# A block of constant products in front of the second head pair's cluster assignment, in place of 16 filling products

## Chip, cores and metric

The kernel runs on one core of a Trainium2 chip. The metric is the device time of one execution in microseconds (us). The kernel before takes 649.86 us (median of 3 executions, 649.46 to 650.00).

## What is computed

Two attentions, one after the other. The first has 4 batches of 8 heads, 768 tokens, head size 64; tokens are assigned to one of 16 clusters by their largest product with normalised centroids, and a query sees only the keys of its own cluster. The second is a causal attention with four experts on the result, of which two are weighted into each token. Cut to what matters here:

```
q_assign = argmax(einsum('bhsd,hcd->bhsc', q_n, c_n), -1)   # k_assign likewise
mask   = q_assign[:, :, :, None] == k_assign[:, :, None, :]
scores = where(mask, scale * q @ k.T, -1e9)
attn   = exp(scores - max(scores)); attn /= sum(attn) + 1e-9
x      = attn @ v                                            # then the four experts on x
```

## The kernel before, in words

The work goes by pairs of heads: 16 pairs of the clustered attention (n = 0 to 15), then 8 of the expert attention. For one pair:

- q and k (tiles `acc`, `xh`, `xl`, `kt`, `qt`, by pair) are loaded and turned so that the head size lies on partitions: by TensorE transposes (L476) for the first pairs, by VectorE transposes (L468) later; ScalarE copies them out (L320) into `xk`, `xq` or, for the second pair, `xh2`, `xh3`.
- **Assignment** (L507): four products of 128 rows and 32 columns of the array write the cluster scores of q and k into one tile of `pp`. VectorE then turns them (L511), takes the maximum, compares and ranks (L518 to L526) and turns back (L514); ScalarE makes rows of it (L531), which go by DMA into `tk`. All of this happens in place in the `pp` tile, so that tile is held until L526 has read it.
- **Row maxima** (L848 products in 64 and 48 rows of the array, two of them side by side; VectorE reduces them at L862): 12 groups of four products for a pair, in two halves of six; each half ends in a small reduce (L868), a turn (L878) and a DMA into `tk`.
- **Scores** (L915), exponentials on ScalarE (L921), sums on GpSimd and VectorE (L325, L326), products with v (L959).

`pp` is PSUM: four slots of two banks each, and every tile of PSUM takes one. `tk0` to `tk2` and `tq0` to `tq2` hold the operands of three pairs in turn.

The order is written out by hand. Work is recorded as numbered operations; the table `ORDER` lists them in the order in which they are issued, each engine runs its own in that order, and `~32` stands for 32 filling products (`spin`, L1103: 128 columns on a tile of ones, result unused). `SLOTS` gives each buffer its slot. In the table before, the filling products stand in rows of 34, 12, 17, 32 and 38 in the first 17 us. The first pair's row maxima begin behind the last of them.

Of the kernel before, what the change touches and what calls it, by code (L numbers as in the profile page):

```python
# [18 lines left out]
FT = mybir.dt.float32  # L19
# [13 lines left out]
          m_add=4, m_moe=0, m_xt=1, enter=4.0)  # L33

ORDER = """
0 4 32 31 33 ~34 1 3 2 56 ~12 8 145 5 10* 9* 13* 6 7 17* 14 ~17 20 18* 34 21 22 37 38 239 36 39 23 35 41 24 147 25 ~32
45 40 28 60 46 11 47 29 15* 27 30 12* 55 48 16* 61 62 42* 44 49 ~38 78 68 79 50 70 76 54 51 71 74 238 69 72 75 57 77
58 89 59 73 52 93 63 91 80 87 81 65* 90 82 88 85 53 43* 94 83 19 86 144 109 84 112 110 92 100 64 159 113 103 333 160
101 98 95 104 163 106 99 164 155 102 107 161 157 146 115 96 158 105 97 240 426 162 108 119 116* 156 111 153 120 332
125 154 117 126 172 118 170 173 122 121 165 131 171 123 128 241 132 124 129 134 166 167 135 136 127 557 137 114 138  # L40
# [99 lines left out]
1220330320332010021313200331111210221220313301322023330012131022133320011001230111020032320323021032032101201203233112  # L140
2210310302011200213321330111301332210023011310023202233323203011102012012133123312010220220122310300323312201003031201
1333331320211101231200030221122002033211201031001230030103301120312022231322011232132200222311300203221210013320231010
3112033030330002212233111133012113001120330010300000000000000000000000010110010101001001010100110010100000000000000000
0000000000000000101010101010101000000000000000000000000000000000000000000000000000000000000000000000000000000000010101
0101010101101010101010101010101010010101010101010101010101010101010101101010101010010101010101010101010100000000000000
0000000000000000000000000000000000000000000000000000000000000000000000000000000000000000000000000000000000000000000000
0000000000000000000000000000000000000000000000000000000000000001201201201201201201201200000000000000000000000000000000
0000000000000000000000000000000000000000000000000000000000000000000000000000000000000000000000000000000000000010101010
1010101010101010000000000000000000000000011000101101011010101010100101110000110100000101000101000000000000000001230123
"""  # L150


# [30 lines left out]
class Plan:  # L183
# [11 lines left out]
    def op(self, eng, dur, fn, due, after=(), use=(), lat=0.0, mode=128, alt=None, at=0.0, port=False):  # L195
        o = Op(eng, dur, fn, due, after, use, lat, mode, alt, at, port)
        self.needs(o, after, use)
        self.ops.append(o)
        return o
# [51 lines left out]
def t_mm(n):  # L251

    return n / 2400 + 0.016
# [13 lines left out]
def kernel(  # L267
# [14 lines left out]
    PE, ACT, DVE, POOL, SP = nc.tensor, nc.scalar, nc.vector, nc.gpsimd, nc.sync  # L282
    B, H, S, D = q.shape
# [4 lines left out]
    HW = S // 2  # L288
# [18 lines left out]
    op = plan.op  # L307

    def dma(dst, src, e=SP):
        e.dma_start(*[x.bitcast(FT) if x.dtype == FR else x for x in (dst, src)])  # L310

    def issues(moves):
        return [(x[0] + 0.045 + 0.05 * (i == 0),) + x[1:] for i, x in enumerate(moves)]

    def banks():
        return plan.buf(psum, "pp", (128, 2, 512), FT, 4)

    def copy_op(dst, src, n, due, after, use, sbuf=False):

        return op("act", t_act(n, sbuf), lambda: ACT.activation(dst(), src(), AF.Copy), due, after, use,  # L320
                  alt=(MO["m_copy"], "dve", t_dve(n), lambda: DVE.tensor_copy(dst(), src())), port=sbuf)  # L321
# [12 lines left out]
    def tmp(tag, shape, dt=FT, bufs=1):  # L334
        return plan.buf(sb, tag, shape, dt, bufs)
# [58 lines left out]
    TK, TQ = [], []  # L394
# [14 lines left out]
    def base(n):  # L409
        return AT["pair"] * min(n, NA) + MO["pair"] * max(n - NA, 0) + \  # L410
            (AT["first"] if n == 0 else AT["second"] if n == 1 else 0.0)
# [654 lines left out]
    def moe_out(b):  # L1066

        n = NA + b * EP + EP - 1
        t1 = base(n) + MO["pair"] + MO["out"]
        wh, wl = W["wo"]  # L1070
        for c in range(NC):
            final = n == NS - 1
            late = final and c >= HC
            m = banks() if c % 2 == 0 else m
            ot = tmp("rb", (128, DM)) if final and c == NC - 1 else tmp("vt" if late else "xt", (128, DM), bufs=2)
            due = base(n) + 40 + c if final else t1 + MO["out_step"] * c
            o = None
            for ep in range(EP):
                d = P[n - EP + 1 + ep]
                if "hl" in d:  # L1080
                    (ah, al_), ready = d["hl"], d["a"][c // HC]
                else:
                    ah, al_, ready = d["a"]

                def go(m=m, c=c, ep=ep, ah=ah, al_=al_):
                    ts = slice(c * 128, (c + 1) * 128)
                    for i, (a_, w_) in enumerate(((ah, wh), (ah, wl), (al_, wh))):
                        PE.matmul(m()[:, c % 2], a_()[:, ts], w_()[:, ep, :], start=(ep == 0 and i == 0),  # L1088
                                  stop=(ep == EP - 1 and i == 2))
                o = op("pe", 3 * t_mm(DM), go, due + 4 * (late and ep == EP - 1), [ready, o] + W["wo_ready"],  # L1090
                       [m, wh, wl, ah, al_, ot])

            o = copy_op(ot, lambda m=m, c=c: m()[:, c % 2], DM, due + 2, [o], [m, ot])

            def go(ot=ot, c=c):
                dma(out[b, c * 128:(c + 1) * 128, :], ot())
            op("sp", issues([(0.36, 0.65, 1.4)]), go, due + 3, [o], [ot])
# [24 lines left out]
    for n in range(NA, NS):  # L1122
# [8 lines left out]
        if ep == 0 and b:  # L1131
            moe_out(b - 1)
    moe_out(B - 1)
    plan.run()


# [26 lines left out]
```

## Time and profile before

| | before |
|---|---|
| median of 3 executions | 649.86 us |
| the profiled execution | 649.03 us |
| its span, first to last instruction | 647.0 us |
| TensorE busy, mean granted clock | 635.7 us, 0.994 |
| VectorE, ScalarE, GpSimd busy | 479.6, 301.1, 457.7 us |

Busy time is what the records cover; idle time of an engine that is not the bound costs nothing. The granted clock is a share of 2.4 GHz: 1.00 is 2.4 GHz, 0.50 is 1.2 GHz. The profiled execution's own time lies 2.03 us above its span. The median lies 0.83 us above the profiled execution.

### The profile page before, as it was taken

How to read it: one execution, taken by the hardware profiler on the slowest of the kernel's cores; microseconds unless marked ns; L12 is line 12 of the kernel's file. 1: busy time of each engine (PE TensorE's matmuls, PEld its weight loads, DVE VectorE, ACT ScalarE, POOL GpSimd, SP SyncE). 2: the span in 40 equal slices, each digit the busy share in tenths (PEclk: the TensorE clock that was granted, in tenths of full speed). 3: DMA queues.
4: the chain of work that ended last, by engine and by line, in shares of the span. 5: the costliest groups of instructions: out<-in, count | busy, mean ns of one | idle time of the engine just before them, and what ended most of it. 6: DMA issues, size and time to landing. Idle time of an engine off the chain costs nothing.

```text
span 647.0 us, 13866 instructions
## 1 busy us (share of the span) xinstructions
PE 635.7 (98%) x5423; PEld 483.4 (75%) x5423; DVE 479.6 (74%) x812; ACT 301.1 (47%) x498; POOL 457.7 (71%) x328
## 2 busy tenths in 40 slices
PE   8899999999999999999999999999999999999997
PEld 7677767567676676676767788779879778878775
DVE  5976967968999687988898874554685567388842
ACT  4355646555365465464555323451451554244423
POOL 3579999999998999889999747974553425051430
PEclk9799999999999999999999999999999999999999
DMA  9755736447312453053352101142011321111233
GB/s 161 161 85 115 123 81 115 99 76 148 96 62 76 111 129 117 26 148 77 117 130 84 51 27 51 50 131 68 2 51 52 100 83 35 45 42 52 68 126 132
DMA packets 128698, 56.62 MB, mean 88 GB/s; under 512 B 110012, under 2 KB 118264, under 8 KB 128632
## 3 DMA queue, kind: packets, MB, share of 16 engines
q1 hardware_dynamic: 126936, 55.23, 34.2%
q8 instruction: 43, 0.70, 0.5%
q10 hardware_dynamic: 1696, 0.49, 0.3%
q14 instruction: 23, 0.19, 0.1%
HBM read 39.49 MB, written 15.86 MB: 86 GB/s over the span
## 4 chain that ended last, share of the span: by engine, by line
PE 85%; POOL 5%; DVE 4%; DMA 2%; issue 2%; ACT 1%; ACTq 0%; SPq 0%; POOLq 0%; DVEq 0%
PE pp L915 25%; PE pp L959 22%; PE pp L641 11%; PE pp L848 9%; PE pp L1088 6%; PE pp L681 5%; POOL acc L325 4%; PE pp L999 3%; PE pp L852 2%; PE pp L507 1%; DVE acc L326 1%; DMA xl<-in_k_dram 1%; ACT p L921 0%; PE pp L476 0%; DVE mx L862 0%
## 5 line engine op out<-in xcount | busy, mean ns | idle before, releaser
L325 POOL TENSOR_TENSOR acc<-acc,p 128x768 f32<-128x768 f32 (+1 forms) x129 | 228.6, 1778 | 25.8 <-DVE acc L326 21.6
L921 ACT ACTIVATE p<-pp 128x768 f32<-128x768 f32 (+2 forms) x264 | 196.3, 773 | 108.5 <-PE pp L915 101.9
L862 DVE TENSOR_REDUCE mx<-pp 128x2 f32<-128x768 f32 (+1 forms) x224 | 204.1, 941 | 56.9 <-PE pp L848 42.8
L915 PE MATMUL pp<-tq,tk 64*128 64x384 f32 (+2 forms) x1584 | 180.4, 333 | 1.5 <-DVE ssb L1006 1.0
L915 PEld LDWEIGHTS pp<-tq,tk 64*128 64x128 f32 x1584 | 135.7, 186 | 21.2 <-issue 10.5
L959 PE MATMUL pp<-p,vt 128*64 128x384 f32 x768 | 130.9, 490 | 0.0
L959 PEld LDWEIGHTS pp<-p,vt 128*64 128x64 f32 x768 | 52.3, 137 | 76.1 <-issue 69.3
L915 PE MATMUL pp<-tk 49*128 49x384 f32 (+2 forms) x528 | 88.5, 329 | 0.0
L325 POOL TENSOR_TENSOR acc<-p,p 128x768 f32<-128x768 f32 (+1 forms) x41 | 74.4, 1817 | 13.4 <-ACT p L921 13.3
L848 PE MATMUL pp<-tk,tq 64*128 64x384 f32 x384 | 70.7, 363 | 2.5 <-DVE tk L321 1.7
L926 POOL TENSOR_SCALAR_AFFINE_SELECT p<-p 128x256 f32<-128x256 f32 x48 | 22.1, 478 | 64.7 <-ACT p L921 64.6
L848 PE MATMUL pp<-tk 48*128 48x384 f32 x384 | 67.6, 344 | 0.0
L848 PEld LDWEIGHTS pp<-tk,tq 64*128 64x128 f32 x384 | 49.0, 250 | 8.9 <-issue 3.3
L320 ACT ACTIVATE avu<-pp 128x384 f32<-128x384 f32 x31 | 15.2, 491 | 77.0 <-PE pp L959 64.5
L915 PEld LDWEIGHTS pp<-tk 49*128 49x128 f32 x528 | 50.5, 185 | 0.0
L848 PEld LDWEIGHTS pp<-tk 48*128 48x128 f32 x384 | 50.2, 253 | 0.3 <-DMA tk<-rows 0.2
L326 DVE TENSOR_TENSOR acc<-acc,p 128x768 f32<-128x768 f32 (+2 forms) x37 | 40.3, 1091 | 3.6 <-POOL acc L325 3.5
L1050 POOL TENSOR_TENSOR xt<-avu,rb 128x384 f32<-128x384 f32 x26 | 31.5, 1235 | 13.1 <-issue 9.4
L860 DVE TENSOR_TENSOR pp<-pp,tri 128x256 f32<-128x256 f32 x48 | 20.5, 427 | 27.2 <-PE pp L852 25.8
L959 PE MATMUL pp<-p,vm 128*64 128x384 f32 (+2 forms) x288 | 39.7, 420 | 0.0
L959 PEld LDWEIGHTS pp<-p,vm 128*64 128x64 f32 x288 | 19.0, 136 | 23.3 <-issue 16.9
L325 POOL TENSOR_TENSOR xl<-vt,xh 128x768 fp32r<-128x768 f32 x10 | 18.6, 1862 | 15.4 <-ACT xh L320 7.6
(197 smaller groups left out, 991.0 us busy)
## 6 DMA issues: line engine op xcount, KB each, us to landing
rb<-rd SPq DMA_DIRECT2D x46, 192.0 KB
x<-xt SPq DMA_DIRECT2D x16, 384.0 KB
out_dram<-xt SPq DMA_DIRECT2D x21, 256.0 KB
vt<-in_v_dram SPq DMA_DIRECT2D x52, 96.0 KB
vt<-x SPq DMA_DIRECT2D x12, 384.0 KB
rw<-rows SPq DMA_DIRECT2D x15, 192.0 KB
tk<-rw SPq DMA_DIRECT2D x30, 96.0 KB
qt<-in_q_dram SPq DMA_DIRECT2D x28, 96.0 KB
```

The lines of the kernel that those rows point to most:

```text
L325: ways = [("pool", t_pool(n), lambda: POOL.tensor_tensor(dst(), a(), b(), op=fn)), ("dve", t_dve(n), lambda: DVE.tensor_tensor(dst(), a(), ...
L326: ("dve", t_dve(n), lambda: DVE.tensor_tensor(dst(), a(), b(), op=fn))]
L641: PE.matmul(m()[:, hf, :HW], w_[:, dc, es], x_[dc]()[:, c], start=(i == 0), stop=(i == 3 * DC - 1))
L681: PE.matmul(m()[:, c % 2, :NV], x_[dc]()[:, ts], w_[:, dc, :], start=(i == 0), stop=(i == 3 * DC - 1))
L848: PE.matmul(ps()[:, h, :HW], at, kt[rs, i * HW:(i + 1) * HW], start=(j == 0), stop=(j == 1))
L862: DVE.tensor_reduce(to, ps()[:, :, :w], axis=AX.X, op=OP.max)
L915: PE.matmul(to, kt[rs, kc * 128:(kc + 1) * 128], by, start=(i == 0), stop=(i == 3))
L921: ACT.activation(pt()[:, :, o_:HW], p()[:, :, o_:HW], AF.Exp, scale=SC)
L926: POOL.affine_select(out=c, in_=c, pattern=[[0, 2], [1, 128]], compare_op=OP.is_ge, fill=0.0, base=0, channel_multiplier=-1)
L959: PE.matmul(av()[h * 64:(h + 1) * 64, 0, o_:HW], d["vv"](h, kc), pt()[:, h, o_:HW], start=(kc == 0), stop=(kc == nk - 1), tile_position=(0 ...
L1050: e.tensor_tensor(xt().rearrange("d (j u f c) -> d f c u j", j=32, u=4, f=2)[:, par], avu()[:, c].rearrange("d (c u j) -> d c u j", c=HC, ...
L1088: PE.matmul(m()[:, c % 2], a_()[:, ts], w_()[:, ep, :], start=(ep == 0 and i == 0), stop=(ep == EP - 1 and i == 2))
```

## The change

The row of 32 filling products ahead of the second pair's assignment becomes 16, and a new operation (number 2496) follows them: 60 products on a constant tile, in four forms. Its operand `wait` is the first 896 columns of `tk2`, set to 0.5 by VectorE early in the program. Its results go to two tiles of `pp` (slots 3 and 1) that nobody reads.

```
 ORDER
-... 147 25 ~32 45 40 28 60 ...
+... 147 25 ~16 2496 45 40 28 60 ...
...
+    wait = TK[2][:, 0, 0:896]
+    DVE.memset(wait.bitcast(FT), 0.5)
+    spare = [banks(), banks()]
+
+    def forms():
+        four = [spare[i // 2]()[:, i % 2] for i in range(4)]
+
+        def rows64(count):
+            for i in range(count):
+                for h in range(2):
+                    rs = slice(h * D, (h + 1) * D)
+                    PE.matmul(four[h][:, :HW], wait[rs, 0:128], wait[rs, 512:896], start=(i == 0), stop=(i == count - 1))
+
+        def rows32(count):
+            for i in range(count):
+                for g in range(4):
+                    rs = slice(g * 32, g * 32 + 32)
+                    PE.matmul(four[g][:, :HW], wait[rs, 0:128], wait[rs, 512:896], start=(i == 0), stop=(i == count - 1))
+
+        def cols64():
+            for h in range(2):
+                PE.matmul(four[0][h * 64:(h + 1) * 64, :128], wait[:, 0:64].bitcast(FT), wait[:, 128:256].bitcast(FT),
+                          start=True, stop=True, tile_position=(0, 64 * h))
+
+        def whole(count):
+            for _ in range(count):
+                PE.matmul(four[1][:, :HW], wait[:, 0:128], wait[:, 512:896], start=True, stop=True)
+        rows64(4)
+        rows32(6)
+        rows64(2)
+        rows32(3)
+        cols64()
+        rows32(2)
+        whole(2)
+    op("pe", 4.0, forms, -1e3, use=spare)
```

(HW is 384, D is 64. `SLOTS` gains the two slots, 3 and 1; its other entries stay and only shift by two places.) All lines below the table move by one, so L507 of the kernel before is L508 of the changed one.

TensorE before, at the second pair's assignment (a tile's first number is its slot of `pp`; what a row waits for stands in brackets by engine or DMA ring):

```order
L1103 MATMUL pp_0_131<-onesb_68 128x128
L507 MATMUL pp_2_325<-xh2_0_279,cbd_89 32x384 [waits PE_49,Activation_49]
L507 MATMUL pp_2_325<-xh2_0_279,cbd_89 32x384
L507 MATMUL pp_2_325<-xh3_0_272,cbd_89 32x384 x2
L476 MATMUL pp_1_333<-identf_80,xl1_0_187 128x128 [waits DMAHW2_49,DMAHW1_49]
```

The assignment waits for ScalarE's copy of the second pair's operand.

TensorE in the changed kernel, at the head of the block:

```order
L1104 MATMUL pp_0_132<-onesb_68 128x128
L1146 MATMUL pp_3_310<-tk2_95 128x384 [waits DVE_49,PE_49]
L1146 MATMUL pp_3_310<-tk2_95 128x384 x7
L1152 MATMUL pp_3_310<-tk2_95 128x384 x2
L1152 MATMUL pp_1_311<-tk2_95 128x384 [waits PE_49,Activation_49]
L1152 MATMUL pp_1_311<-tk2_95 128x384
```

The block's first tile takes slot 3, in which the first pair's assignment (`pp_3_248` here, `pp_3_247` before) lies; the wait on VectorE is for the last reader of that tile, the compare at L526 of the first pair.

TensorE in the changed kernel, at the block's end:

```order
L1156 MATMUL pp_3_310<-tk2_95 64x128 x2
L1152 MATMUL pp_3_310<-tk2_95 128x384 x2
L1152 MATMUL pp_1_311<-tk2_95 128x384 x2
L1152 MATMUL pp_3_310<-tk2_95 128x384 x2
L1152 MATMUL pp_1_311<-tk2_95 128x384 x2
L1161 MATMUL pp_3_310<-tk2_95 128x384 x2
L508 MATMUL pp_2_372<-xh2_0_280,cbd_89 32x384 [waits PE_49]
```

The second pair's assignment now stands behind the whole block. On VectorE one row is new; ScalarE, GpSimd and the DMA queues keep their rows and their order.

## Rows read from the trace of the kernel before

**Rows 1.** The page: busy time by engine, and TensorE's granted clock in 40 slices.

```profile
PE 635.7 (98%) x5423; PEld 483.4 (75%) x5423; DVE 479.6 (74%) x812; ACT 301.1 (47%) x498; POOL 457.7 (71%) x328
...
PEclk9799999999999999999999999999999999999999
```

**Rows 2.** Chain of waits, first 60 us: start, length, engine and what.

```profile
19.79 3.58 DMA xl<-in_k_dram
...
27.92 1.83 DVE mx L862 x2
...
29.89 2.62 PE pp L915 x23
```

**Rows 3.** Timeline of TensorE, 8 to 20 us: start, length, instruction, idle before.

```profile
11.31 1.95 PE L1103 MATMUL pp<-onesb 128*128 128x128 bf16 x32
13.21 0.85 PE L507 MATMUL pp<-xh,cbd 128*32 128x384 f32 x8
13.99 0.87 PE L476 MATMUL pp<-identf,xl 128*128 128x128 f32 x6
14.70 2.29 PE L1103 MATMUL pp<-onesb 128*128 128x128 bf16 x38
18.73 0.51 PE L848 MATMUL pp<-tk,tq 64*128 64x384 f32 x2 [1.74 <-DVE tk L321]
```

**Rows 4.** Windows: length, busy us (instructions) by engine, granted clock, DMA share, GB/s.

```profile
18.73:21.72 2.99, 2.94 (x19) 2.46 (x20) 2.77 (x5) 0.71 (x1) 2.97 (x3) 0.98 0.41 94
21.72:28.40 6.68, 6.46 (x34) 4.77 (x31) 5.93 (x9) 3.00 (x4) 2.69 (x3) 0.50 0.88 188
...
28.40:647.00 618.60, 611.34 (x5194) 463.23 (x5192) 460.01 (x767) 289.07 (x476) 445.22 (x309) 1.00 0.33 84
```

**Rows 5.** Timeline of VectorE, 12 to 34 us.

```profile
13.17 0.56 DVE L526 TENSOR_TENSOR oh<-pp,sm 128x384 bf16<-128x384 f32 x1
...
15.16 0.98 DVE L468 STREAM_TRANSPOSE xq<-qt 128x768 f32<-128x768 f32 x1 [0.83 <-DMA qt<-in_q_dram]
16.07 0.56 DVE L511 STREAM_TRANSPOSE pp<-pp 128x384 f32<-128x384 f32 x1
...
18.32 0.35 DVE L321 CAST tk<-xk 128x384 fp32r<-128x384 f32 x1
...
20.27 0.92 DVE L862 TENSOR_REDUCE mx<-pp 128x2 f32<-128x768 f32 x1
21.34 4.41 DVE L862 TENSOR_REDUCE mx<-pp 128x2 f32<-128x768 f32 x5 [0.15 <-PE pp L848]
...
26.33 0.91 DVE L862 TENSOR_REDUCE mx<-pp 128x2 f32<-128x768 f32 x1
27.92 4.42 DVE L862 TENSOR_REDUCE mx<-pp 128x2 f32<-128x768 f32 x5 [0.68 <-PE pp L848]
```

**Rows 6.** Timeline of TensorE: pairs of products in 64 and 48 rows, at either clock.

```profile
26.08 0.52 PE L848 MATMUL pp<-tk 48*128 48x384 f32 x2
26.40 0.52 PE L848 MATMUL pp<-tk,tq 64*128 64x384 f32 x2
...
35.18 0.34 PE L848 MATMUL pp<-tk,tq 64*128 64x384 f32 x2
35.36 0.34 PE L848 MATMUL pp<-tk 48*128 48x384 f32 x2
```

**Rows 7.** Chain of waits, 45 to 53 us: where TensorE's form changes.

```profile
45.92 0.78 PE pp L507 x8
...
50.73 0.90 PE pp L915 x8
...
51.98 0.70 PE pp L915 x8
```

**Rows 8.** Timeline, 7 to 8 us: VectorE's idle time early on.

```profile
7.59 1.02 DVE L321 COPY xq<-pp 128x384 f32<-128x384 f32 x2 [2.12 <-PE pp L476]
```

**Rows 9.** Waits of TensorE, whole span: us in total, times, longest; the longest after 30 us.

```profile
PE pp L999 <- POOL acc L325: 1.2, 1, 1.2
```

More of the change, by code (lines that the diff above doesn't have):

```diff
@@ L35 @@
 ORDER = """
-0 4 32 31 33 ~34 1 3 2 56 ~12 8 145 5 10* 9* 13* 6 7 17* 14 ~17 20 18* 34 21 22 37 38 239 36 39 23 35 41 24 147 25 ~32
-45 40 28 60 46 11 47 29 15* 27 30 12* 55 48 16* 61 62 42* 44 49 ~38 78 68 79 50 70 76 54 51 71 74 238 69 72 75 57 77
+0 4 32 31 33 ~34 1 3 2 56 ~12 8 145 5 10* 9* 13* 6 7 17* 14 ~17 20 18* 34 21 22 37 38 239 36 39 23 35 41 24 147 25 ~16
+2496 45 40 28 60 46 11 47 29 15* 27 30 12* 55 48 16* 61 62 42* 44 49 ~38 78 68 79 50 70 76 54 51 71 74 238 69 72 75 57 77
 58 89 59 73 52 93 63 91 80 87 81 65* 90 82 88 85 53 43* 94 83 19 86 144 109 84 112 110 92 100 64 159 113 103 333 160
@@ L142 @@
 1333331320211101231200030221122002033211201031001230030103301120312022231322011232132200222311300203221210013320231010
-3112033030330002212233111133012113001120330010300000000000000000000000010110010101001001010100110010100000000000000000
-0000000000000000101010101010101000000000000000000000000000000000000000000000000000000000000000000000000000000000010101
-0101010101101010101010101010101010010101010101010101010101010101010101101010101010010101010101010101010100000000000000
+3112033030330002212233111133012113001120330010331000000000000000000000000101100101010010010101001100101000000000000000
+0000000000000000001010101010101010000000000000000000000000000000000000000000000000000000000000000000000000000000000101
+0101010101011010101010101010101010100101010101010101010101010101010101011010101010100101010101010101010101000000000000
 0000000000000000000000000000000000000000000000000000000000000000000000000000000000000000000000000000000000000000000000
-0000000000000000000000000000000000000000000000000000000000000001201201201201201201201200000000000000000000000000000000
-0000000000000000000000000000000000000000000000000000000000000000000000000000000000000000000000000000000000000010101010
-1010101010101010000000000000000000000000011000101101011010101010100101110000110100000101000101000000000000000001230123
+0000000000000000000000000000000000000000000000000000000000000000012012012012012012012012000000000000000000000000000000
+0000000000000000000000000000000000000000000000000000000000000000000000000000000000000000000000000000000000000000101010
+1010101010101010100000000000000000000000000110001011010110101010101001011100001101000001010001010000000000000000012301
+23
 """
```

## Prediction

> **What bounds the kernel now.** The page comes first: TensorE is busy 98% of the span, and its granted clock falls only at the span's beginning [rows 1]. The windows show that one fall exactly: the clock is 0.50 (1.2 GHz) from 21.72 to 28.40 us and 1.00 (2.4 GHz) from there to the end [rows 4]. Half of those 6.68 us, 3.34 us, is therefore the most that a steadier clock can give back. After 30 us TensorE waits for next to nothing: its longest wait there is 1.2 us in all, for GpSimd [rows 9]. So a delay that reaches the first scores (L915, at 29.89 us) is carried to the end, and the change, which touches only the first 14 us, is worth what it moves that start.
>
> The chain of waits before that start runs through the load of `xl`, TensorE and two reduces of VectorE [rows 2]. VectorE's own timeline tells more. From the second pair's turn (L511, 16.07 us) to the sixth reduce it works almost without a gap: the only waits are 0.15 us before the second reduce and 0.68 us before the eighth, both for TensorE [rows 5]. VectorE is thus the bound of this stretch, and TensorE comes second with 0.83 us of slowness that shows. At 16.07 us L511 does not wait for TensorE, since the second pair's assignment (L507) ends at 13.21 + 0.85 = 14.06 us [rows 3]; VectorE waits for a load, then turns `xq` [rows 5]. The assignment has 2.0 us of slack.
>
> **The block's start.** The 16 products that go cost 16 x 1.95/32 = 0.98 us [rows 3]; they only fill the wait for ScalarE, so their removal gives nothing. The rest end at 12.28 us. The block cannot begin then: its first tile takes slot 3, which the first pair's compare (L526) reads until 13.17 + 0.56 = 13.73 us [rows 5]. With 0.04 us for the hand-over it begins at 13.77 us, after 1.5 us of new idle time. The second slot needs ScalarE's copy of `xh2`, the same that lets L507 start at 13.21 us before the change [rows 3]; it is not later.
>
> **The block's length.** It has 6 rounds of two products in 64 rows, 11 rounds of four in 32 rows, two products in 64 columns and two whole ones.
> - A pair in 64 rows takes 35.36 - 35.18 = 0.18 us at full clock [rows 6]. Six are 1.08 us.
> - No row shows four products in 32 rows. If the four run side by side, a round costs a pair's 0.18 us, since each streams the same 384 columns; if only two do, 0.36 us. I take 0.18 us, because the assignment shows four column strips side by side: eight instructions of 384 columns in 0.78 us [rows 7]. That is 1.98 us; the other end is 3.96 us.
> - The two products in 64 columns have a third of the assignment's columns: 0.78/3 = 0.26 us [rows 7]. The two whole ones are at most 0.18 us each, 0.36 us.
> - The form changes six times from the first row group to the assignment. Behind products in all rows, the first group of L915 takes 0.90 us against 0.70 us otherwise [rows 7], so a change costs up to 0.20 us; none shows into L507. I take 0.10 us each, 0.6 us in all, between 0 and 1.2.
>
> The sum is 1.08 + 1.98 + 0.26 + 0.36 + 0.6 = 4.28 us, with bounds 3.7 and 6.9 us.
>
> The Trainium skill ("TensorE: Matmul & The Clock Gate", Part 3, measured speedup) gives four products of 32 rows a gain of 3.07, not 4. By that rule a round would cost 0.18 x 4/3.07 = 0.23 us, the block 0.6 us more, and the time would be 652.6 us; no run here shows it yet.
>
> **What waits behind it.** Everything on TensorE is queued behind the block. It ends at 13.77 + 4.28 = 18.05 us, the assignment 0.85 us later at 18.90 [rows 3], and L511 starts at about 18.92 instead of 16.07: VectorE's dense chain is 2.85 us late. Next on TensorE come the transposes (0.87 us) and 38 filling products (2.29 us) [rows 3], until 22.05 us. The first row maxima then start 0.5 us after their operand (the cast at 18.32 + 0.35 [rows 5], plus 2.85); the reduces hide that, since the first is due only at 20.27 + 2.85 = 23.12 us.
>
> Given back are VectorE's waits. TensorE now has several groups ready when the reduces begin, so the 0.15 us goes. The 0.68 us goes too if the clock is full there: four groups of 0.36 us then fit easily into VectorE's pace. At half clock a pair takes 26.40 - 26.08 = 0.32 us [rows 6], and some 0.2 us of it stays. The load of `xl`, in the chain before [rows 2], is ahead of the delay and lands in time. The start of L915 moves by 2.85 - 0.83 = 2.0 us, or 2.2 us with the clock at half. I take 2.1 us.
>
> The new memset on VectorE has 896 columns; by a reduce of 768 columns in 0.92 us [rows 5] it takes at most 1.1 us. VectorE is idle for 2.12 us before its next copy [rows 8], so it costs nothing; without that cover it would be the whole 1.1 us. `tk2` is written by the real third pair only after the row maxima have begun, behind the block.
>
> **The sum.** The profiled execution is 649.03 us (span 647.0 and 2.03 us around it); with 2.1 us it becomes 651.1. The median of the runs is 0.83 us above that execution, so the median becomes 652.0 us. About 0.2%, 1.3 us, can be told from no change. With the block between 3.7 us and 4.9 us (all six form changes at 0 or at 0.20), the forecast's own range is 651.3 to 652.8.
>
> **The rivals.**
> 1. *Not slower: the clock gives back more than the block takes.* The block keeps TensorE dense from 13.77 to 22 us, where it was idle for 1.74 us before the row maxima [rows 3]. If that idle time is what took the clock down at 21.72, and TensorE, not VectorE, is what sets the pace of the 6.68 us, then 3.34 us comes back against 2.85 us: 649.86 - 0.5 = 649.4 us, and 648.8 with the shortest block. The deciding point is whether TensorE ends the stretch. For it: TensorE is busy 6.46 of 6.68 us there. Against it: VectorE is busy 5.93 of them [rows 4] and waits 0.68.
> 2. *The clock falls already in the block.* Before the change the fall came 2.99 us after an idle stretch of 1.74 us, with the engine busy for 2.94 of them [rows 3, 4]. The new idle stretch of 1.5 us ends at 13.77 us; the same distance puts a fall at 16.8 us. The last 1.3 us of the block and the assignment's 0.85 would double: 2.1 us more, 654.1 us. [...] Against it, the new gap is the shorter one.
> 3. *The fall moves later.* The row maxima remain as sparse as they were. If the clock falls some 6 us later than before, its 6.68 us lie mostly in the scores, where TensorE is the bound: half of that, 3.3 us, is added, 655.3 us.
> 4. *Two at a time in 32 rows.* 11 x 0.18 = 2.0 us more: 654.0 us.
> 5. *The change does not keep the clock up at all.* Then the fall stays where it is, and the time is the forecast's upper half, 652.2 us; it is counted with the forecast.
>
> **How the numbers follow.** The forecast has 0.52, rival 1 has 0.22 (0.16 within 0.2%, 0.06 below), rival 2 has 0.12, rival 3 has 0.06, rival 4 has 0.08. Slower by over 0.2% are the forecast and rivals 2 to 4: 0.78. The range reaches from 650.6, which takes in the shortest block with a little luck in the clock and the upper part of rival 1, to 654.8, which takes in rivals 2 and 4. Left out are most of rival 1 and rival 3, about 0.2.
>
> **What would show it.** Right: TensorE idle from about 12.3 to 13.8 us, released by L526; the block some 4.3 us long; L511 near 18.9 us with TensorE as its releaser; the wait of 1.74 us before the row maxima gone; L915 starting near 32 us; nothing different after that but the shift. Rounds in 32 rows of 0.36 us would show rival 4, a clock of 0.50 before 20 us rival 2, one beyond 32 us rival 3. The forecast is wrong if the block starts at 12.3 us, if it takes under 3 us, or if L915 starts before 31 us.

## The result, and the profile after

The changed kernel takes 654.79 us (median of 3 executions, 652.91 to 654.80) against 649.86: a ratio of 1.0068, with a 95% interval of 1.004 to 1.0095. It is slower, by 4.9 us where 2.1 were forecast, and 654.79 lies just inside the range. Six more executions beside 26 of the kernel before gave a smaller distance: 653.64 against 650.49 us, a ratio of 1.0058 (1.0038 to 1.0078). In all, the kernel before ran 82 times (mean 650.2 us, 648.25 to 652.24) and the changed one 9 times (mean 653.9, 652.66 to 655.16). **The change costs about 3.7 us**; the interval of 1.0038 to 1.0078 is 2.5 to 5.1 us. Single executions of the kernel before differ by up to 4.0 us, those of the changed one by up to 2.5.

The page after, the lines that answer to [rows 1]:

```profile
PE 641.0 (98%) x5469; PEld 487.4 (75%) x5469; DVE 481.4 (74%) x813; ACT 301.2 (46%) x498; POOL 457.9 (70%) x328
...
PEclk9989999999999999999999999999999999999999
```

The span is 652.9 us, 5.9 more than before. The timeline of TensorE after, at the place of [rows 3]:

```profile
13.47 1.06 PE L1104 MATMUL pp<-onesb 128*128 128x128 bf16 x16
16.04 0.97 PE L1146 MATMUL pp<-tk 64*128 64x384 f32 x8 [1.51 <-DVE oh L527]
16.94 1.32 PE L1152 MATMUL pp<-tk 32*128 32x384 f32 x24
18.20 0.62 PE L1146 MATMUL pp<-tk 64*128 64x384 f32 x4
18.74 0.80 PE L1152 MATMUL pp<-tk 32*128 32x384 f32 x12
19.47 0.44 PE L1156 MATMUL pp<-tk 128*64 128x128 f32 x4
19.84 0.62 PE L1152 MATMUL pp<-tk 32*128 32x384 f32 x8
20.39 0.62 PE L1161 MATMUL pp<-tk 128*128 128x384 f32 x2
20.94 0.85 PE L508 MATMUL pp<-xh,cbd 128*32 128x384 f32 x8
21.73 0.87 PE L477 MATMUL pp<-identf,xl 128*128 128x128 f32 x6
22.44 2.29 PE L1104 MATMUL pp<-onesb 128*128 128x128 bf16 x38
24.73 0.51 PE L849 MATMUL pp<-tk,tq 64*128 64x384 f32 x2
```

The block waits 1.51 us for the first pair's compare (L527, L526 before) and lasts 20.94 - 16.04 = 4.90 us. The idle time of 1.74 us before the row maxima [rows 3] is gone. VectorE after, against [rows 5]:

```profile
15.34 0.56 DVE L527 TENSOR_TENSOR oh<-pp,sm 128x384 bf16<-128x384 f32 x1
...
21.93 0.60 DVE L512 STREAM_TRANSPOSE pp<-pp 128x384 f32<-128x384 f32 x1 [4.57 <-PE pp L508]
...
26.18 5.25 DVE L863 TENSOR_REDUCE mx<-pp 128x2 f32<-128x768 f32 x6
31.46 0.17 DVE L869 TENSOR_REDUCE M<-mx 128x6 fp32r<-128x12 f32 x1
31.66 0.44 DVE L879 STREAM_TRANSPOSE tm<-M 128x192 f32<-128x192 f32 x1
31.99 5.23 DVE L863 TENSOR_REDUCE mx<-pp 128x2 f32<-128x768 f32 x6
```

The second pair's turn (L512) now waits 4.57 us for TensorE; the waits of 0.15 and 0.68 us are gone and the twelve reduces stand without a gap. The windows after, with the columns of [rows 4]:

```profile
21.00:24.00 3.00, 3.00 (x43) 2.36 (x43) 1.96 (x4) 0.87 (x2) 0.00 (x0) 1.00 0.56 128
24.00:27.70 3.70, 3.36 (x33) 2.65 (x30) 3.63 (x7) 0.71 (x1) 3.04 (x3) 1.00 0.38 123
27.70:31.00 3.30, 2.78 (x20) 1.89 (x20) 3.30 (x5) 1.17 (x3) 1.11 (x2) 1.00 0.72 145
31.00:34.50 3.50, 2.54 (x20) 1.68 (x18) 3.43 (x6) 1.83 (x2) 2.88 (x2) 0.99 0.32 64
34.50:37.50 3.00, 2.73 (x17) 2.76 (x19) 2.72 (x4) 1.04 (x2) 0.71 (x1) 0.50 0.88 214
```

The clock stays at 2.4 GHz through the row maxima and falls to 1.2 GHz at 34.5 us, as the first scores begin. In the chain of waits those scores start 4.88 us later than before (29.89 us, [rows 2]):

```profile
34.77 3.77 PE pp L916 x24
```

One difference lies ahead of the block. TensorE in the first 12 us, before:

```profile
6.06 0.83 PE L1103 MATMUL pp<-onesb 128*128 128x128 bf16 x12 [0.60 <-ACT cbd L390]
6.73 1.48 PE L476 MATMUL pp<-identf,acc 128*128 128x128 f32 x12
...
9.09 0.59 PE L507 MATMUL pp<-xk,cbd 128*32 128x384 f32 x2
```

and after:

```profile
6.21 1.44 PE L1104 MATMUL pp<-onesb 128*128 128x128 bf16 x12 [0.60 <-ACT cbd L391]
7.45 2.77 PE L477 MATMUL pp<-identf,acc 128*128 128x128 f32 x12
...
11.32 0.52 PE L508 MATMUL pp<-xk,cbd 128*32 128x384 f32 x2
```

The same products take almost twice as long after, at half clock, and the first assignment starts 11.32 - 9.09 = 2.23 us late. (The granted clock reads 1.00 there in both; the durations tell it.) The rest of the span adds up: L512 is 5.86 us late, which is 2.2 from this beginning, 2.85 as forecast and 0.8 more; the scores are 4.88 late, 0.98 having come back on VectorE; and three groups of scores at half clock add 1.1. (The beginning reaches L512 in full here: from the first assignment to L512 it is 10.61 us, and 10.67 us in the early run of this kernel with denser row maxima, below.)

### The profile page after: what moved, and what is told of

The parts are those of the page before. It is cut to its first block, busy times and chain, and to the rows that moved or that the text cites. A ratio compares the mean times of both kernels' runs of the same rounds, so it can differ in the third digit from the quotient of the medians.

```text
span 652.9 us, 13962 instructions
## 1 busy us (share of the span) xinstructions
PE 641.0 (98%) x5469; PEld 487.4 (75%) x5469; DVE 481.4 (74%) x813; ACT 301.2 (46%) x498; POOL 457.9 (70%) x328
## 4 chain that ended last, share of the span: by engine, by line
PE 89%; DVE 5%; POOL 3%; issue 1%; ACT 1%; ACTq 0%; DVEq 0%
PE pp L916 27%; PE pp L960 23%; PE pp L642 11%; PE pp L849 9%; PE pp L1089 6%; PE pp L682 5%; PE pp L1000 3%; PE pp L853 2%; POOL acc L326 2%; DVE mx L863 2%; PE pp L508 2%; DVE acc L327 1%; PE pp L1104 0%; PE pp L477 0%; PE pp L1152 0%
## 5 line engine op out<-in xcount | busy, mean ns | idle before, releaser
L916 PEld LDWEIGHTS pp<-tq,tk 64*128 64x128 f32 x1584 | 137.2, 187 | 20.9 <-issue 10.5
L849 PE MATMUL pp<-tk 48*128 48x384 f32 x384 | 65.8, 337 | 0.0
L327 DVE TENSOR_TENSOR acc<-acc,p 128x768 f32<-128x768 f32 (+2 forms) x37 | 41.8, 1133 | 3.7 <-POOL acc L326 3.5
```

The source lines that it names most:

```text
L327: ("dve", t_dve(n), lambda: DVE.tensor_tensor(dst(), a(), b(), op=fn))]
L849: PE.matmul(ps()[:, h, :HW], at, kt[rs, i * HW:(i + 1) * HW], start=(j == 0), stop=(j == 1))
L916: PE.matmul(to, kt[rs, kc * 128:(kc + 1) * 128], by, start=(i == 0), stop=(i == 3))
```

## Experiments

The theory behind the first runs: the block delays the second pair's assignment and VectorE's chain one to one; its excess length is changes of form; the late beginning is chance. Rivals: the memset or the program causes the late beginning, products in 32 rows are slow, the idle time on TensorE takes the clock down. Medians are given with the ratio to the kernel before on the same chip and its interval.

**The changed kernel again** (no edit).

> The changed kernel once more. Its profile showed the products of the first 11 us at half clock for some 5 us longer than the kernel before (the first assignment at 11.32 instead of 9.09 us). Theory A: that is chance, the moment at which the clock rises differs from execution to execution. Then the times fall into two groups some 2 us apart (near 652.9 and near 654.8 us), and the kernel before shows both groups as well in enough executions. Theory B: the change itself (its memset, its code) causes it. Then nearly all executions of the changed kernel lie near 654.8 us and none of the kernel before is 2 us above its median.

653.64 us, 652.66 to 655.16; the kernel before beside it 648.29 to 652.24 in 26 executions. Both kernels spread by 2.5 to 4 us, without two clean groups, and none of the 26 lies 2 us above its median, so these times do not decide. Profiles do: this one has the late beginning (first assignment at 11.13 us), but so have two below without memset and block (11.04 us each). The change is not needed for it; theory A. The two groups appear in two later variants: 651.7 to 652.3 and 653.7 to 654.1 us with the free slot, 652.4 to 652.6 and 654.2 to 654.5 us with denser row maxima. The profiled execution of the first is of the upper group and began late (first assignment at 10.89 us), that of the second is of the lower group and began early (9.09 us).

This profile has no fall of the clock at all, at nearly the same beginning, and so gives the price of the fall by itself (VectorE's timeline, then the chain of waits):

```profile
21.74 0.60 DVE L512 STREAM_TRANSPOSE pp<-pp 128x384 f32<-128x384 f32 x1 [4.56 <-PE pp L508]
...
34.57 2.61 PE pp L916 x23
```

From L512 to the scores it is 12.83 us, as in the first profile (34.77 - 21.93 = 12.84). The scores at the head of the chain then take 2.61 us instead of 3.77, and from L512 to the end of the span it is 629.8 us instead of 630.9. The fall cost 1.1 us.

**The memset alone**

```
+    wait = TK[2][:, 0, 0:896]
+    DVE.memset(wait.bitcast(FT), 0.5)
     plan.run()
```

> The kernel before with only the new memset on VectorE; the 32 filling products stay and there is no block. Theory A (chance): the same time as the kernel before within 0.5 us in executions of equal beginning, since VectorE is idle for 2.12 us there; a beginning that is 2 us late in some. Theory B (the memset delays the beginning): 2 us slower in all, the first assignment near 11.3 us.

650.11 us, ratio 1.0003 (0.9988 to 1.0018), first assignment at 9.24 us. The memset costs nothing that can be told, and did not make the beginning of this profile late.

**A free slot for the block's first tile**

```
 SLOTS (the two entries of the block's tiles)
-31
+21
```

> The changed kernel with the block's first tile in slot 2, which is free when ScalarE has copied the second pair's operand, instead of slot 3, which the first pair's compare holds. If the hand-over of slot 3 costs time on the path: the idle time before the block falls from 1.5 us to about 0.9 us, everything behind it moves 0.5 to 0.6 us earlier, and the time falls by 0.5 us. If VectorE's chain is held by something else: no difference.

652.31 us, 1.0039 (1.0023 to 1.0056). The block now waits for ScalarE:

```profile
14.63 0.98 PE L1146 MATMUL pp<-tk 64*128 64x384 f32 x8 [0.45 <-ACT xh L321]
```

From the first assignment's start to L512 it is 20.68 - 10.89 = 9.79 us, against 21.93 - 11.32 = 10.61: 0.8 us less. The held slot was on the path, and for somewhat more than expected. (The trace shows this; the intervals of the two times overlap.)

**One form**

```
-        rows64(4)
-        rows32(6)
-        rows64(2)
-        rows32(3)
-        cols64()
-        rows32(2)
-        whole(2)
+        rows64(19)
```

> The block as 19 rounds of two products in 64 rows only, 38 products in place of 60, about the same time on the array, without the changes of form in between. If a change of form costs 0.18 to 0.19 us, as the trace of the changed kernel reads: the block takes 3.6 us in place of 4.90, and the time falls by 1.3 us less what the clock does. If the products in 32 rows are what costs (0.21 us a round): 19 x 0.18 + 0.2 = 3.6 us as well, but then the rounds inside a run of equal form in the changed kernel would stand 0.21 us apart, not 0.18.

```profile
16.00 3.60 PE L1146 MATMUL pp<-tk 64*128 64x384 f32 x38 [1.51 <-DVE oh L527]
19.53 0.85 PE L508 MATMUL pp<-xh,cbd 128*32 128x384 f32 x8
```

The block takes 3.53 us. L512 comes 20.52 - 11.29 = 9.23 us behind the first assignment, 1.4 us less than in the changed kernel. The median, 653.35 us (650.25 to 653.85; 1.0038, 1.0022 to 1.0054), hides it, since 7 of the 12 executions lie near 653.6, as the profiled one does, which began late; the mean is 652.6, 1.3 us under the changed kernel's. The intervals of the times overlap here too, so it is the trace that shows the gain. In the changed kernel the runs of 6, 3 and 2 rounds in 32 rows stand 1.26, 0.73 and 0.55 us from the start of the next, so a round costs 0.18 us and what is over is 0.19: the change of form.

**Sixteen fills less, no block**

```
-... 147 25 ~32
+... 147 25 ~16
```

> The kernel before with 16 filling products in place of 32 and no block and no memset. If the removed products only filled a wait, as the prediction has it: the assignment still starts when ScalarE's copy is there, and the time is that of the kernel before within 0.5 us, so the block alone makes the change slower. If the removed products kept the clock up: the clock falls earlier or for longer than in the kernel before, and the time rises by up to 1 us.

650.94 us, 1.0008 (0.9997 to 1.002). The removed products cost at most little; the block carries the change. The profile has the late beginning (first assignment at 11.04 us) without any block; of its 1.95 us, 1.01 reach L511 here (17.08 us).

**The block twice**

```
+        for _ in range(2):
             rows64(4)
...
             whole(2)
```

> The changed kernel with the block's 60 products issued twice. If TensorE, and behind it VectorE's chain, carry the block one to one to the end: the assignment, L512 and the first scores move by 4.9 us more, and the time lies 4.9 us above the changed kernel (near 658.5 us). If later slack takes part of a delay: clearly less than 4 us.

658.30 us, 1.0124 (1.0106 to 1.0143): 4.7 us above the changed kernel's median, or 4.5 when each mean is taken against the kernel before beside it (8.0 and 3.5 us). This execution began early (first assignment at 9.08 us, L512 at 24.69 us), and its L512 stands 4.93 us behind that of the run with one block that began equally early (19.76 us, the denser row maxima in the changed kernel, below). From L512 to the scores it is again 12.84 us (37.53 - 24.69), so the delay is carried to the scores one to one. The last step, to the end, is less exact: the clock falls here too, from 36 to 42.5 us, which is longer than in the changed kernel.

**The idle time filled**

```
-... 44 49 ~38 78
+... 44 49 ~66 78
```

> The kernel before with 66 in place of 38 filling products ahead of the first row maxima, so that TensorE does not stand idle for the 1.74 us there; no block. Theory A (the idle time takes the clock down): the fall to 0.50 during the row maxima disappears, and up to 0.8 us is gained. Theory B (the sparse row maxima take it down): a fall still comes in the row maxima or in the first scores, in most executions, and the time is within 0.5 us of the kernel before, or above it when the fall moves into the scores.

650.41 us, 0.9996 (0.9984 to 1.0008). The 1.74 us of idle time are 0.17, and the clock falls all the same, later and for less time (24.3 to 27.7 us instead of 21.7 to 28.4):

```profile
18.00:21.00 3.00, 2.70 (x21) 1.98 (x20) 2.93 (x6) 0.87 (x3) 2.25 (x2) 1.00 0.20 48
21.00:24.00 3.00, 1.84 (x17) 1.32 (x14) 2.71 (x4) 0.47 (x1) 1.89 (x3) 1.00 1.01 236
24.00:27.70 3.70, 3.40 (x18) 3.10 (x20) 3.41 (x6) 1.80 (x4) 0.02 (x1) 0.54 1.01 199
```

The mean clock is 0.997 or less in all 12 executions, so the fall does not need the idle time; theory B. TensorE is busy 1.84 of 3 us in the row maxima ahead of the fall.

**Fills at the beginning**

```
-0 4 32 31 33 ~34 1 3 2 56 ~12 8
+0 4 32 31 33 ~37 1 2496 3 2 56 ~12 8
...
+    gap = banks()
+    def spin_gap():
+        for _ in range(6):
+            PE.matmul(gap()[:, 1, HW:], onesb, onesb, start=True, stop=True)
+    op("pe", 0.6, spin_gap, -1e3, use=[gap])
```

> The kernel before with 3 more filling products ahead of the centroids' transpose and 6 in a PSUM slot of their own behind it, so that TensorE is not idle between 4.85 and 6.06 us. If that idle time decides when the clock rises first: the executions in which the first assignment is 2 us late disappear, the times draw together near 649 us, and the mean falls by about 1 us (the kernel before had 648.3 to 652.2 us in 26 executions). If the moment of the rise is set elsewhere: the spread stays as it is.

650.39 us (649.86 to 652.49), 1.0009 (0.9998 to 1.0021). The idle time shrank to 0.27 us, the spread stayed (2.6 us, against 2.9 for the kernel before beside it) and the mean (650.7) did not fall. This is the second case of the expectation: nothing shows that this idle time decides when the clock first rises.

**Denser row maxima in the changed kernel**

```
                     def go(hf=hf, i=i, cc=cc, w=w, ps=ps):
+                        if n == 0:
+                            for _ in range(2):
+                                for h in range(2):
+                                    rs = slice(h * D, (h + 1) * D)
+                                    at = qh[rs, hf * HW + cc:(hf + 1) * HW:HC]
+                                    PE.matmul(ps()[:, h, :HW], at, kh[rs, i * HW:(i + 1) * HW], start=True, stop=True)
```

> The changed kernel with the first pair's row maxima made denser on TensorE: each of the 12 groups first issues four products more (two pairs, 0.36 us at full clock) into its own PSUM tile, which the real products then overwrite. A group takes 0.72 us, still under VectorE's 0.92 us. Theory (the sparse row maxima take the clock down, and in the changed kernel the fall then lies in the first scores): the fall in the scores disappears, mean clock near 1.00, and the time falls by 0.5 to 1.2 us against the changed kernel (653.6 us). Rival (the fall has another cause, or the extra products cost as much): the same time or 0.3 us more, and a clock still at 0.997.

652.54 us, 1.0046 (1.0028 to 1.0064), mean clock 0.999 or 1.000 in all 7 executions, where it is 0.997 or less in 8 of the 9 of the changed kernel. The fall in the scores is gone:

```profile
31.00:34.00 3.00, 2.84 (x28) 2.32 (x28) 2.76 (x4) 0.40 (x1) 2.80 (x2) 1.00 0.29 61
34.00:37.00 3.00, 3.00 (x34) 2.65 (x32) 2.42 (x4) 2.48 (x4) 0.00 (x0) 1.00 0.99 214
```

The median lies 1.1 us under the changed kernel's, the mean 0.9, but the intervals overlap, and 5 of these 7 executions belong to the group of lower times, the profiled one among them. The trace says less. The extra products hold up the scores:

```profile
33.51 0.79 PE L922 MATMUL pp<-tq,tk 64*128 64x384 f32 x6
```

That is 13.75 us behind L512, against 12.84 in the changed kernel. From L512 to the end of the span it is 630.6 us, against 630.9: of the 1.1 us that the fall costs, 0.3 came back. The run shows what takes the clock down, and not its price. With the early beginning (first assignment at 9.09 us, as in the kernel before) this profile shows the block's delay by itself:

```profile
19.76 0.60 DVE L512 STREAM_TRANSPOSE pp<-pp 128x384 f32<-128x384 f32 x1 [3.45 <-PE pp L508]
```

That is 3.69 us behind 16.07 [rows 5].

**Denser row maxima in the kernel before** (the same edit)

> The same denser row maxima in the kernel before. If sparse row maxima take the clock down: no fall between 21 and 28 us, mean clock above 0.997, and 0 to 0.8 us gained, less up to 0.4 us by which the first group comes later. If the 1.74 us of idle time ahead of them does: the fall stays, and the extra products then cost 0.64 us a group at half clock, so the time rises by 1 us or more.

650.22 us, 1.0002 (0.9991 to 1.0013), mean clock 0.999 or 1.000 in 8 of 12 executions and 0.997 in four; in the kernel before it is 0.997 or less in 77 of 79. The fall in the row maxima is gone in this profile, and no time is gained: TensorE now waits 1.08 us for the load of `xl` in this stretch, and VectorE waits 0.84 and 1.18 us for TensorE. So this run does not show that the fall was free. The 79 executions point the other way: the two with a mean clock of 1.000 took 648.25 and 648.58 us, the 24 with 0.997 on average 649.7, the 33 with 0.994 on average 650.6. Whether the clock itself makes that difference, or the beginning or the loads that go with it, no run here tells.

**The block moved** (in one form, and with one tile of `pp` in place of two)

```
-... 147 25 ~16 2496 45 ... 44 49 ~38 78
+... 147 25 ~32 45 ... 44 49 2496 78
...
+        rows64(20)
```

> A block of 20 rounds of two products in 64 rows (3.6 us) put where TensorE has time: in place of the 38 filling products behind the second pair's transposes, with the 32 filling products ahead of the assignment as in the kernel before. If it is the place, ahead of the assignment, that makes the change slower: the time is that of the kernel before within 0.5 us, with L511 where it was. If products in rows of 64 cost by themselves, by their clock or by reading the tile: 1 us slower or more.

649.82 us, 0.9993 (0.9978 to 1.0008), L512 at 16.47 us with a beginning 0.14 us late. In the place where TensorE had time, 3.77 us of such products cost nothing that can be told, and gain nothing. No version here beats the kernel before by more than its interval.

## Why the prediction was right, and where its sizes were off

- **Start of the block: right.** It waits for the first pair's compare; 1.51 us of idle time against 1.5 forecast. The hand-over took 0.14 us, not 0.04.
- **Length: mis-sized by one term.** Rounds of four in 32 rows cost 0.18 us as taken, so rival 4 is out. The Trainium skill ("TensorE: Matmul & The Clock Gate", Part 3, measured speedup) has a gain of 3.07 for four products in 32 rows. By that figure a round would take an estimated 0.23 us, and inside a run of rounds the trace shows 0.18. (With the changes of form spread over these short runs, the 11 rounds take 1.26 + 0.73 + 0.55 = 2.54 us, 0.23 each as well; but that is a cost for each run of rounds, not for each round.) The step that was off is "I take 0.10 us each" for six changes of form: with the one into the assignment, taken as nothing, there are seven, and six of the seven cost 0.18 to 0.19 us (about 0.1 is left for the 64 columns). 4.90 us against 4.28 is that, and one form brought it down to 3.53.
- **VectorE as the bound: right.** L512 is late by what TensorE is late; 0.98 us came back on it, 0.83 forecast. From L512 to the scores it is 12.83 or 12.84 us in all five profiles with a block ahead of the assignment and the row maxima as they were. Without such a block it varies: 13.82 us in the profile that the prediction read, 14.26 to 15.51 in the five others with the same row maxima. So that profile showed less of VectorE's waits than the kernel before mostly has. Two blocks moved L512 by 4.9 us and the time by 4.5 to 4.7.
- **Free removals and the memset: right** within the intervals (no block 1.0008, memset 1.0003).
- **Rival 1 fell:** the clock stayed up through the row maxima and gave back no more than VectorE's gaps.
- **Rival 2 did not occur** in any profile with the block, and its reason is not needed: with the idle time filled the clock goes down all the same, though later.
- **Rival 3, at 0.06, is what happened**, in four of five profiles with a block ahead of the assignment and the row maxima as they were (not in the repeated run). It cost 1.1 us, not 3.3, since the clock was back by 38 us. In the kernel before, the fall lies in row maxima that VectorE and a load set the pace of. The change moves it to where TensorE is the bound. What the fall cost in its old place is not shown; in the profile before it is at most the 0.98 us that came back.
- **That the first result lies in the range is luck:** 654.79 is 0.01 us inside its upper end, which was set there for rivals 2 and 4, and neither of them occurred. 2.2 us of that result are the late beginning. The mean of the nine executions, 653.9 us, lies inside without such luck, but with 1.1 us of rival 3 in it, which the range was meant to leave out.

The sum as measured: 3.69 us of delay at L512 with equal beginnings, less the 0.98 that came back, with 1.1 for the fall in the scores, gives 3.8, against 3.7 from the means. The terms are from single profiles and the mean is uncertain by over 1 us, so the sum is no closer than that. Against the forecast's 2.85 us, the 3.69 hold 0.6 more for the forms and 0.2 more for the two hand-overs. The 4.9 of the first comparison holds the chance of the beginning in addition: the profile of the changed kernel began late, that of the kernel before early, and the prediction took the one it saw as the kernel's. What decides the beginning stays open: 6 of the 13 profiles are late, with and without the block, and filling the idle time did not change the spread. Four of the six with a block ahead of the assignment are late and two of the seven others; so few cannot tell whether the change makes it likelier, and a part of the 3.7 us may be that.

## What to carry to other kernels

Work that only fills time must stand where the engine has time behind it as well as ahead of it, and its buffers must be free then: here it took a PSUM slot that VectorE still read, ahead of the one step that VectorE's chain waited for. Keep such a block in one form of the array. Ask where a fall of the clock lies before counting it as a loss: 6.7 us at half clock showed as at most 0.98 us where VectorE set the pace, and some 3 us of it cost 1.1 us where TensorE did. Whatever delays a stretch can move the fall from the one place to the other.

## What the runs showed of the hardware

- Four products in 32 rows, two in 64 and one in 128 rows of the array, 384 columns each, all cost 0.18 us a round inside a run of equal rounds; in this block, going from one form to another cost 0.18 to 0.19 us in six of seven cases, also from 64 to 32 rows.
- The clock fell to 1.2 GHz behind short groups of products with waits between them (TensorE busy 1.84 of 3 us), without the longer idle stretch ahead of them. With the groups made dense the mean clock was 0.999 or 1.000 in 15 of 19 executions. The short groups do not always bring a fall: the repeated run of the changed kernel had none.
- An execution begins at half clock, for a time that differs: the same 12 products took 0.83 us at 6.06 us in the kernel before and 1.44 us at 6.21 us in the changed one, whose products became fast only at about 10 us. That moved the first assignment by up to 2.2 us, also between executions without the change. The first three executions of the kernel before span 0.5 us and do not show it; all 82 span 4 us.
